# x of the first half stored as its two parts: the low part formed at the eviction in attention, four loads more, one exponential buffer fewer

## The chip, the cores and the metric

One core of one Trainium2 chip runs the whole kernel in one launch. The metric is the device time in microseconds (us) of an execution, the median of three runs unless said otherwise. The engines are TensorE (PE; PEld is its weight load), VectorE (DVE), ScalarE (ACT), GpSimd (POOL) and SyncE (SP). SP does nothing here but issue DMAs, in the order in which they are written; ACT issues a few as well.

## The reference, cut to what matters

```
scores = scale * q @ k.T                        # 4 batches, 12 heads, 448 x 448, head width 64
scores = einsum('bhij,hg->bgij', scores, w_pre)
attn = softmax(scores, axis=-1)
attn = einsum('bhij,hg->bgij', attn, w_post)
x = (attn @ v) as 1792 tokens x 768
h = ((x @ w1) * (x @ w2)) @ w3 @ w_out          # width 1024
out = relu(h @ w_in) ** 2 @ w_out2              # width 2048
```

All of it is float32. The kernel keeps that precision on TensorE by splitting an operand into a rounded high part and a low part (the operand less its high part) and adding three products, high with high, high with low and low with high.

## The kernel before, in words

**Attention.** The rows of the 4 batches are cut into 16 chunks n of 110, 110, 110 and 118 rows, and these into 180 blocks g of up to 10 rows with all 12 heads (120 partitions). A step d of the program handles two blocks, 2d and 2d+1. For them `regroup` loads r (the scores of a block, by a DMA that SP issues two steps ahead), `premix` multiplies r by the mixing weights into PSUM (sp, two buffers, so a step's premix waits until the exponentials of the step before have read theirs), `rowmax` on DVE finds the negated maximum nm, `expo` on ACT takes the exponential p with its sum sm, POOL and DVE turn the sum into a factor (`norm_add`, `norm_recip`), `p_hi` on ACT and `p_lo` on DVE (one step later) make the two halves ph and pl, `tmix` on PE mixes heads (two steps later), and its result is evicted into p2 by ACT (`p2_act`, every fourth block) or DVE (`p2_dve`). When all blocks of chunk n are there, `pv` multiplies by v: two results per chunk, y = 0 and 1, two or three steps apart, in one PSUM buffer. In the step after, `pv_out` on ACT copies the result into a tile xs (three buffers) and SP stores it into xd, a scratch tensor in DRAM that holds x.

The order is written out by hand: `ORDER` lists what each engine does in a step, one line per engine.

```
    ORDER = (
        ("premix", "scores", "tmix", "pv"),
        ("expo", "evac", "p_hi", "p2_act", "pv_out", "high_q"),
        ("rowmax", "p_lo", "norm_recip", "p2_dve", "high_k"),
        ("norm_add", "low_q", "low_k"),
    )
```

**The tail and the layers behind it.** The layers use x in halves of two batches; the first half is chunks n = 0 to 7, with a tile pair (x0h, x0l) for each of its two batches t. The last steps of attention (the tail, numbered by half steps from step 82, `TAIL`) fetch and split the first weights and also x of the first half: `load_x` loads xd into x0l, two chunks in each DMA, and `split_x` makes x0h on ACT (L695) and subtracts it on POOL (L697), in place. For batch t = 1 both come in the last steps. `early` runs the first layer's products of batch 0 on PE between the last steps (e). The second half is loaded and split much later, and the change leaves that as it is.

Of the kernel before, what the change touches and what calls it, by code (L numbers as in the profile page):

```python
# [20 lines left out]
IC = 118  # L21
# [15 lines left out]
def fused_kernel(ctx, tc, q, k, v, w_pre, w_post, w1, w2, w3t, wo, win, wo2, eye, out):  # L37
# [7 lines left out]
    dram = ctx.enter_context(tc.tile_pool(name="dram", bufs=1, space=bass.MemoryType.DRAM))  # L45
    xd = dram.tile([B, 128, 6, S], F, name="xd")
    w34d = dram.tile([6, 128, 8, 128], F, name="w34d")
    w12d = dram.tile([2, 8, 128, DM], F, name="w12d")
# [113 lines left out]
    class Attention:  # L162
        def __init__(self, const, ka, kb, kc, ps):
# [4 lines left out]
            self.nm, self.sm, self.tp, self.p2 = {}, {}, {}, {}  # L168
            self.v, self.pvt = {}, {}
            c = const  # L170
# [31 lines left out]
        def setup_post(self):  # L202
            kw, kab, ones = (self.kc.tile([120, S], F, tag="p", name=x, bufs=5) for x in ("kw", "kab", "ones"))
            kw, kab = (x[:, :120].rearrange("p (g i) -> p g i", i=10) for x in (kw, kab))
# [119 lines left out]
        def expo(self, g):  # L324
            kk = 12 * blocks[g][4]
            if g % 2 == 0:
                self.sm[g // 2] = self.kc.tile([120, 2], F, tag="sm", name=f"sm{g}", bufs=3)
            p = self.kc.tile([120, S], F, tag="p", name=f"p{g}", bufs=5)
            nc.scalar.activation(  # L329
                p[:kk], self.sp.pop(g)[:kk], AF.Exp, bias=self.nm.pop(g)[:kk],  # L330
                accum_out=self.sm[g // 2][:kk, g % 2 : g % 2 + 1],
            )
            self.pt[g] = p
# [103 lines left out]
        def pv_out(self, n, y):  # L437
            o, ic, _ = CHUNKS[n % 4]
            t = self.pvt.pop((n, y))
            u = self.kb.tile([128, 3, IC], F, tag="xs", name=f"xs{n}_{y}", bufs=3)  # L440
            for z, w in ((0, ic),) if ic % 10 == 0 else ((0, 109), (109, 9)):
                nc.scalar.activation(u[:, :, z : z + w], t[:, :, z + z % 10 // 9 : z + z % 10 // 9 + w], AF.Copy)
            eng = nc.sync if n < 15 else nc.scalar
            eng.dma_start(xd[n // 4, :, 3 * y : 3 * y + 3, o : o + ic], u[:, :, :ic])


    TAIL = {
        "w": (-6, -5, -4, -3, 3, 5, 7, 9, 11, 13, 15), "n": (-1, 1, 3, 5, 7, 9, 11, 13, 17),
        "x": (-12, 4), "xn": (0, 11), "h": 8, "hn": 2,
    }  # L450

    def attention_plan():
# [32 lines left out]
        ("expo", "evac", "p_hi", "p2_act", "pv_out", "high_q"),  # L485
        ("rowmax", "p_lo", "norm_recip", "p2_dve", "high_k"),
        ("norm_add", "low_q", "low_k"),
    )
    NEEDS = {
        "rowmax": "premix", "expo": "rowmax", "evac": "scores", "norm_add": "expo", "norm_recip": "norm_add",  # L490
        "p_hi": "norm_recip", "p2_act": "tmix", "p2_dve": "tmix",
    }
# [4 lines left out]
    }  # L497
    AFTER = {"pv_out": "pv", "low_q": "high_q", "low_k": "high_k"}

# [27 lines left out]
    class Moe:  # L527
# [76 lines left out]
        def tail_plan(self):  # L604
# [3 lines left out]
            def at(t, f):  # L608
                ev.setdefault(t, []).append(f)

            for i in range(11):
# [3 lines left out]
                if i < 8:  # L615
                    for part in range(2):
                        at(TAIL["n"][i] + 2, lambda i=i, part=part: w.join(i, part))
                    at(TAIL["n"][i] + 4, lambda i=i: (w.place(i), w.high(i), w.save(i, self.keep[i]), w.rest(i)))
            for u in range(8):
                at(TAIL["x"][u // 4] + 2 * (u % 4), lambda u=u: self.load_x(0, u))  # L620
                at(TAIL["xn"][u // 4] + 2 * (u % 4), lambda u=u: self.split_x(0, u))
            return ev

        def early(self, i, psum):

            ws = [self.w.out[2 * i + j] for j in range(2)]
            xh, xl = self.xy["x", 0, 0]
            assert all((0, u) in self.ready for u in range(4))
            acc = psum(i)
            terms = [(self.chunk(ws, c), (xh[:, c], xl[:, c])) for c in range(6)]  # L630
            for c in range(6):
                yield mm3(acc, terms[c : c + 1], c == 0, c == 5)
            self.acc[i] = acc

        def begin(self, ap_):
            self.ap = ap_

            for c in range(8):
# [30 lines left out]
        def new_xy(self, name, t, parts="hl"):  # L669
            out = []  # L670

            for e, lead, size in (("h", 16, 32), ("l", 48, 96)) if t else (("h", 56, 104), ("l", 24, 32)):
                if e not in parts:
# [6 lines left out]
        def load_x(self, hf, u):  # L680
            t, u4 = divmod(u, 4)
            if u4 == 0:
                part = hf == 0 and t == 0
                self.xy["x", hf, t] = (None, *self.new_xy("x0", t, "l")) if part else self.new_xy(f"x{hf}", t)
            if u4 % 2 == 0:
                w = slice(CHUNKS[u4][0], sum(CHUNKS[u4 + 1][:2]))
                nc.sync.dma_start(f32(self.xy["x", hf, t][1][:, :, w]), xd[2 * hf + t, :, :, w])

        def split_x(self, hf, u):
            t, u4 = divmod(u, 4)  # L690
            o, ic, _ = CHUNKS[u4]
            if self.xy["x", hf, t][0] is None:
                self.xy["x", hf, t] = (*self.new_xy(f"x{hf}", t, "h"), self.xy["x", hf, t][1])
            xh, xl = (x[:, :, o : o + ic] for x in self.xy["x", hf, t])
            nc.scalar.activation(xh, f32(xl), AF.Copy)  # L695
            eng = nc.gpsimd if u % 2 or not hf else nc.vector
            eng.tensor_tensor(xl, f32(xl), f32(xh), ALU.subtract)  # L697
            self.ready.add((hf, u))

# [345 lines left out]
```

## Time and profile before

| what | before |
|---|---|
| median of 3 runs, us | 1312.99 (1311.14 to 1314.83) |
| time of the profiled execution, us | 1316.63 |
| its span, first to last instruction, us | 1314.7 |
| PE busy | 1284.7 us, 98% of the span |
| DVE, ACT, POOL busy | 64%, 55%, 36% |
| granted TensorE clock, mean | 0.996 |

The profiled execution lies 3.6 us above the median, within some 2 us of the slowest of the runs. Its span leaves 1.9 us outside the first and the last instruction. Attention takes the first 460 us of it, the layers the rest. Times in the profile's rows count from the start of the span.

### The profile page before, as it was taken

Reading aid. Unit: us, or ns where it says so; the run is one execution under the profiler, and the core shown is the slowest. Engines: PE = TensorE matmul, PEld = TensorE weight load, DVE = VectorE, ACT = ScalarE, POOL = GpSimd, SP = SyncE. Lnnn points to the kernel's source line nnn. Section 1 sums busy time; section 2 is a strip of 40 time slices with the busy share of each in tenths; the row PEclk is TensorE's granted clock in tenths of the full one; section 3 lists DMA queues with packets and bytes.
Section 4 is the critical chain, followed back from the end, with each engine's and each line's share of the span. In section 5 each row is a group of like instructions: output and inputs, shape, how many; then the busy total and the mean of one; then the engine's idle time right before and its main releaser. Section 6 shows DMA issues by size and latency. Waiting matters only on the chain.

```text
span 1314.7 us, 23355 instructions
## 1 busy us (share of the span) xinstructions
PE 1284.7 (98%) x8542; PEld 1112.2 (85%) x8542; DVE 845.5 (64%) x1535; ACT 716.8 (55%) x1587; POOL 472.8 (36%) x528
## 2 busy tenths in 40 slices
PE   7999999999998999999999999999999999999998
PEld 3677777776766798999999999999999999999998
DVE  4889888889788676643127734769665337735742
ACT  5988889888886565443224533534344225534530
POOL 4354264255324512002222322236776322322331
PEclk9999999999998999999999999999999999999999
DMA  6566576566566567655123432472221223433441
GB/s 213 166 182 191 135 204 205 138 189 204 141 176 185 166 210 219 226 160 153 56 81 108 144 109 75 125 230 91 82 73 48 72 85 111 158 93 86 127 146 52
DMA packets 99399, 184.51 MB, mean 140 GB/s; under 512 B 20949, under 2 KB 68053, under 8 KB 98773
## 3 DMA queue, kind: packets, MB, share of 16 engines
q1 hardware_dynamic: 86928, 172.98, 44.4%
q10 hardware_dynamic: 12357, 10.04, 2.3%
q8 instruction: 67, 1.10, 0.3%
q14 instruction: 47, 0.39, 0.1%
HBM read 124.01 MB, written 20.45 MB: 110 GB/s over the span
## 4 chain that ended last, share of the span: by engine, by line
PE 83%; issue 4%; DVE 4%; DMA 3%; ACT 3%; POOL 2%; SPq 0%; ACTq 0%; POOLq 0%; DVEq 0%
PE l L57 39%; PE y L57 9%; PE sp L315 8%; PE tp L380 5%; PE p L57 5%; PE pv L432 5%; PE sc L289 4%; DMA r<-s 1%; DVE pl L371 1%; DMA kraw<-k 1%; POOL wl L142 1%; ACT ph L355 1%; DVE p L394 1%; DVE nm L321 1%; ACT p L329 1%
## 5 line engine op out<-in xcount | busy, mean ns | idle before, releaser
L142 POOL TENSOR_TENSOR wl<-f,wh 128x384 fp32r<-128x384 f32 (+1 forms) x144 | 166.3, 1155 | 467.2 <-ACT wh L114 446.9
L98 DVE TENSOR_SCALAR f<-y 128x384 int32<-128x384 int32 (+1 forms) x176 | 135.1, 767 | 87.7 <-ACT y L86 86.0
L315 PE MATMUL sp<-r,kpre 120*120 120x448 f32 x360 | 159.8, 565 | 11.4 <-ACT p L329 7.0
L329 ACT ACTIVATE p<-sp,nm 120x448 f32<-120x448 f32 x180 | 113.6, 642 | 49.7 <-DVE nm L321 49.5
L57 PE MATMUL l<-bhh,wh 128*128 128x448 f32 x384 | 139.3, 363 | 0.0
L57 PE MATMUL l<-blh,wh 128*128 128x448 f32 x384 | 138.8, 362 | 0.0
L57 PE MATMUL l<-bhh,wl 128*128 128x448 f32 x384 | 138.7, 361 | 0.0
L371 DVE SCALAR_TENSOR_TENSOR pl<-p,sm,ph 120x448 f16<-120x448 f32 (+3 forms) x270 | 137.6, 563 | 0.3 <-POOL ph L357 0.3
L321 DVE TENSOR_REDUCE nm<-sp 120x1 f32<-120x448 f32 x180 | 107.5, 617 | 42.3 <-PE sp L315 37.7
L114 ACT ACTIVATE wh<-f 128x384 fp32r<-128x384 f32 (+1 forms) x160 | 89.9, 562 | 75.6 <-DVE f L100 68.7
L100 DVE SCALAR_TENSOR_TENSOR f<-raw,f 128x384 int32<-128x384 int32 (+1 forms) x176 | 124.5, 707 | 6.0
L380 PEld LDWEIGHTS <-ph 120*128 120x128 f16 x1260 | 93.7, 99 | 31.9 <-issue 23.9
L355 ACT ACTIVATE ph<-p,sm 120x448 f16<-120x448 f32 (+1 forms) x180 | 107.8, 664 | 17.5 <-DVE sm L349 16.0
L380 PE MATMUL tp<-kwh,ph 120*128 120x120 f16 x630 | 107.0, 218 | 4.5 <-DVE p L396 2.3
L380 PE MATMUL tp<-kwh,pl 120*128 120x120 f16 x630 | 106.1, 217 | 0.0
L380 PE MATMUL tp<-kwl,ph 120*128 120x120 f16 x630 | 106.1, 217 | 0.0
L315 PEld LDWEIGHTS sp<-r,kpre 120*120 120x120 f32 x360 | 59.3, 185 | 54.9 <-issue 19.9
L86 ACT ACTIVATE y<-raw 128x384 f32<-128x384 f32 (+1 forms) x176 | 102.9, 585 | 0.7 <-DMA raw<-w 0.6
L289 PE MATMUL sc<-kt,qh 128*110 128x448 f32 (+1 forms) x192 | 98.4, 512 | 2.2 <-DVE kt L253 1.4
L344 POOL TENSOR_SCALAR sm<-sm 120x2 f32<-120x2 f32 (+3 forms) x94 | 24.7, 263 | 204.9 <-ACT p L329 200.4
L895 ACT ACTIVATE r<-l 128x448 f32<-128x448 f32 x64 | 34.9, 545 | 110.2 <-PE l L57 110.2
L300 ACT ACTIVATE s<-sc 110x448 f32<-110x448 f32 (+1 forms) x186 | 90.5, 559 | 6.2 <-PE sc L289 6.0
(622 smaller groups left out, 3280.9 us busy)
## 6 DMA issues: line engine op xcount, KB each, us to landing
r<-s SPq DMA_DIRECT2D x172, 210.0 KB
raw<-win SPq DMA_DIRECT2D x64, 384.0 KB
raw<-wo SPq DMA_DIRECT2D x48, 512.0 KB
raw<-w SPq DMA_DIRECT2D x32, 384.0 KB
kraw<-k SPq DMA_DIRECT2D x24, 448.0 KB
raw<-w3t SPq DMA_DIRECT2D x16, 512.0 KB
qraw<-q SPq DMA_DIRECT2D x35, 220.0 KB
v<-v SPq DMA_DIRECT2D x4, 1536.0 KB
```

What stands on the lines that cost most here:

```text
L57: nc.tensor.matmul(acc, w, x, start=(first and i == 0 and j == 0), stop=(last and i == n - 1 and j == 2), skip_group_check=again,)
L86: nc.scalar.activation(y, self.raw[i][:, :, 1].bitcast(F), AF.Prelu, scale=2.0**-112, alpha=-(2.0**32))
L98: nc.vector.tensor_scalar(fi, yi, 3, None, ALU.logical_shift_left)
L100: nc.vector.scalar_tensor_tensor(fi, raw[:, :, 0], 29, fi, ALU.logical_shift_right, ALU.bitwise_or)
L142: eng.tensor_tensor(self.out[i][1], self.ft.pop(i), f32(self.out[i][0]), ALU.subtract)
L289: nc.tensor.matmul(sc[:ic], t[:, hh * ic : hh * ic + ic], self.kt[b, h // 2][:, h % 2], start=(i == 0), stop=(i == 1))
L315: nc.tensor.matmul(t[:kk], self.kpre[:kk, :kk], self.rt.pop(g)[:kk], start=True, stop=True)
L321: nc.vector.tensor_reduce(nm[:kk], self.sp[g][:kk], AX.X, ALU.max, negate=True)
L329: nc.scalar.activation(p[:kk], self.sp.pop(g)[:kk], AF.Exp, bias=self.nm.pop(g)[:kk], accum_out=self.sm[g // 2][:kk, g % 2 : g % 2 + 1],)
L355: nc.scalar.activation(h[:, to], p[:, fr], AF.Copy, scale=sm)
L371: nc.vector.scalar_tensor_tensor(l[:, to], p[:, fr], sm, h[:, to], ALU.mult, ALU.subtract)
L380: nc.tensor.matmul(t[:, j], p[:, at : at + 128], w, start=(i == 0), stop=(i == 2))
```

## The change: what it does

For n below 8 `pv_out` writes the rounded high part into xs and a new `pv_lo` on DVE subtracts it from the PSUM result and so makes the low part; SP stores the high part into xd and the low part into a new scratch tensor xld. `pv_lo` is last in DVE's line of the step, and in chunks of 118 rows it takes two instructions, as `pv_out` does. An xs tile now holds both parts (two buffers instead of three). `split_x` is gone for the first half; `load_part` loads x0l from xld and x0h from xd, eight DMAs instead of four, at new places in the tail. The exponentials p have four buffers instead of five. (L numbers in the rows of after are some 1 to 20 higher for the same code.)

```diff
@@ -44,6 +44,7 @@
 
     dram = ctx.enter_context(tc.tile_pool(name="dram", bufs=1, space=bass.MemoryType.DRAM))
     xd = dram.tile([B, 128, 6, S], F, name="xd")
+    xld = dram.tile([B // 2, 128, 6, S], F, name="xld")
     w34d = dram.tile([6, 128, 8, 128], F, name="w34d")
     w12d = dram.tile([2, 8, 128, DM], F, name="w12d")
 
@@ -166,7 +167,7 @@
             self.kt, self.kraw, self.qraw, self.qh, self.ql = {}, {}, {}, {}, {}
             self.st, self.rt, self.sp, self.pt = {}, {}, {}, {}
             self.nm, self.sm, self.tp, self.p2 = {}, {}, {}, {}
-            self.v, self.pvt = {}, {}
+            self.v, self.pvt, self.xs = {}, {}, {}
             c = const
             self.eye = c.tile([120, 10], F, name="eye")
             self.w2a = c.tile([120, 12], F, name="w2a")
@@ -200,7 +201,7 @@
 
 
         def setup_post(self):
-            kw, kab, ones = (self.kc.tile([120, S], F, tag="p", name=x, bufs=5) for x in ("kw", "kab", "ones"))
+            kw, kab, ones = (self.kc.tile([120, S], F, tag="p", name=x, bufs=4) for x in ("kw", "kab", "ones"))
             kw, kab = (x[:, :120].rearrange("p (g i) -> p g i", i=10) for x in (kw, kab))
             ones = ones[:, :128]
             nc.vector.memset(ones, 1.0)
@@ -325,7 +326,7 @@
             kk = 12 * blocks[g][4]
             if g % 2 == 0:
                 self.sm[g // 2] = self.kc.tile([120, 2], F, tag="sm", name=f"sm{g}", bufs=3)
-            p = self.kc.tile([120, S], F, tag="p", name=f"p{g}", bufs=5)
+            p = self.kc.tile([120, S], F, tag="p", name=f"p{g}", bufs=4)
             nc.scalar.activation(
                 p[:kk], self.sp.pop(g)[:kk], AF.Exp, bias=self.nm.pop(g)[:kk],
                 accum_out=self.sm[g // 2][:kk, g % 2 : g % 2 + 1],
@@ -436,17 +437,30 @@
 
         def pv_out(self, n, y):
             o, ic, _ = CHUNKS[n % 4]
-            t = self.pvt.pop((n, y))
-            u = self.kb.tile([128, 3, IC], F, tag="xs", name=f"xs{n}_{y}", bufs=3)
-            for z, w in ((0, ic),) if ic % 10 == 0 else ((0, 109), (109, 9)):
-                nc.scalar.activation(u[:, :, z : z + w], t[:, :, z + z % 10 // 9 : z + z % 10 // 9 + w], AF.Copy)
+            t = self.pvt[n, y]
+            u = self.xs[n, y] = self.kb.tile([128, 2, 3, IC], R, tag="xs", name=f"xs{n}_{y}", bufs=2)
+            for to, fr in self.held(n):
+                nc.scalar.activation((u if n < 8 else f32(u))[:, 0, :, to], t[:, :, fr], AF.Copy)
             eng = nc.sync if n < 15 else nc.scalar
-            eng.dma_start(xd[n // 4, :, 3 * y : 3 * y + 3, o : o + ic], u[:, :, :ic])
+            eng.dma_start(xd[n // 4, :, 3 * y : 3 * y + 3, o : o + ic], f32(u[:, 0, :, :ic]))
+
+        def held(self, n):
+            if n % 4 < 3:
+                return [(slice(0, 110), slice(0, 110))]
+            return [(slice(0, 109), slice(0, 109)), (slice(109, 118), slice(110, 119))]
+
+        def pv_lo(self, n, y):
+            o, ic, _ = CHUNKS[n % 4]
+            t, u = self.pvt.pop((n, y)), self.xs.pop((n, y))
+            if n < 8:
+                for to, fr in self.held(n):
+                    nc.vector.tensor_tensor(u[:, 1, :, to], t[:, :, fr], f32(u[:, 0, :, to]), ALU.subtract)
+                nc.sync.dma_start(xld[n // 4, :, 3 * y : 3 * y + 3, o : o + ic], f32(u[:, 1, :, :ic]))
 
 
     TAIL = {
         "w": (-6, -5, -4, -3, 3, 5, 7, 9, 11, 13, 15), "n": (-1, 1, 3, 5, 7, 9, 11, 13, 17),
-        "x": (-12, 4), "xn": (0, 11), "h": 8, "hn": 2,
+        "x": (-12, 0, 6, 10), "h": 8, "hn": 2,
     }
 
     def attention_plan():
@@ -483,19 +497,19 @@
     ORDER = (
         ("premix", "scores", "tmix", "pv"),
         ("expo", "evac", "p_hi", "p2_act", "pv_out", "high_q"),
-        ("rowmax", "p_lo", "norm_recip", "p2_dve", "high_k"),
+        ("rowmax", "p_lo", "norm_recip", "p2_dve", "high_k", "pv_lo"),
         ("norm_add", "low_q", "low_k"),
     )
     NEEDS = {
         "rowmax": "premix", "expo": "rowmax", "evac": "scores", "norm_add": "expo", "norm_recip": "norm_add",
-        "p_hi": "norm_recip", "p2_act": "tmix", "p2_dve": "tmix",
+        "p_hi": "norm_recip", "p2_act": "tmix", "p2_dve": "tmix", "pv_lo": "pv_out",
     }
 
     LAG = {
         "premix": 0, "tmix": 2, "p2_act": 2, "p2_dve": 2, "rowmax": 0, "expo": 0,
         "norm_add": 0, "norm_recip": 0, "p_hi": 0, "p_lo": 1,
     }
-    AFTER = {"pv_out": "pv", "low_q": "high_q", "low_k": "high_k"}
+    AFTER = {"pv_out": "pv", "pv_lo": "pv", "low_q": "high_q", "low_k": "high_k"}
 
     def attention_step(A, d, ev):
         now, before = ev.get(d, {}), ev.get(d - 1, {})
@@ -616,16 +630,17 @@
                     for part in range(2):
                         at(TAIL["n"][i] + 2, lambda i=i, part=part: w.join(i, part))
                     at(TAIL["n"][i] + 4, lambda i=i: (w.place(i), w.high(i), w.save(i, self.keep[i]), w.rest(i)))
-            for u in range(8):
-                at(TAIL["x"][u // 4] + 2 * (u % 4), lambda u=u: self.load_x(0, u))
-                at(TAIL["xn"][u // 4] + 2 * (u % 4), lambda u=u: self.split_x(0, u))
+            for t in range(2):
+                for k, e in enumerate("lh"):
+                    for u in range(2):
+                        at(TAIL["x"][2 * t + k] + 2 * u, lambda t=t, u=u, e=e: self.load_part(t, u, e))
             return ev
 
         def early(self, i, psum):
 
             ws = [self.w.out[2 * i + j] for j in range(2)]
-            xh, xl = self.xy["x", 0, 0]
-            assert all((0, u) in self.ready for u in range(4))
+            xl, xh = self.xy["x", 0, 0]
+            assert all((0, u, e) in self.ready for u in range(2) for e in "hl")
             acc = psum(i)
             terms = [(self.chunk(ws, c), (xh[:, c], xl[:, c])) for c in range(6)]
             for c in range(6):
@@ -634,6 +649,8 @@
 
         def begin(self, ap_):
             self.ap = ap_
+            for t in range(2):
+                self.xy["x", 0, t] = self.xy["x", 0, t][::-1]
 
             for c in range(8):
                 for e in range(2):
@@ -669,7 +686,7 @@
         def new_xy(self, name, t, parts="hl"):
             out = []
 
-            for e, lead, size in (("h", 16, 32), ("l", 48, 96)) if t else (("h", 56, 104), ("l", 24, 32)):
+            for e, lead, size in (("h", 48, 96), ("l", 16, 32)) if t else (("h", 56, 104), ("l", 24, 32)):
                 if e not in parts:
                     continue
                 p = self.pre if t == 0 and e == "l" else self.wp
@@ -680,22 +697,18 @@
         def load_x(self, hf, u):
             t, u4 = divmod(u, 4)
             if u4 == 0:
-                part = hf == 0 and t == 0
-                self.xy["x", hf, t] = (None, *self.new_xy("x0", t, "l")) if part else self.new_xy(f"x{hf}", t)
+                self.xy["x", hf, t] = self.new_xy(f"x{hf}", t)
             if u4 % 2 == 0:
                 w = slice(CHUNKS[u4][0], sum(CHUNKS[u4 + 1][:2]))
                 nc.sync.dma_start(f32(self.xy["x", hf, t][1][:, :, w]), xd[2 * hf + t, :, :, w])
 
-        def split_x(self, hf, u):
-            t, u4 = divmod(u, 4)
-            o, ic, _ = CHUNKS[u4]
-            if self.xy["x", hf, t][0] is None:
-                self.xy["x", hf, t] = (*self.new_xy(f"x{hf}", t, "h"), self.xy["x", hf, t][1])
-            xh, xl = (x[:, :, o : o + ic] for x in self.xy["x", hf, t])
-            nc.scalar.activation(xh, f32(xl), AF.Copy)
-            eng = nc.gpsimd if u % 2 or not hf else nc.vector
-            eng.tensor_tensor(xl, f32(xl), f32(xh), ALU.subtract)
-            self.ready.add((hf, u))
+        def load_part(self, t, u2, e):
+            if u2 == 0:
+                self.xy["x", 0, t] = (*self.xy.get(("x", 0, t), ()), *self.new_xy("x0", t, e))
+            w = slice(CHUNKS[2 * u2][0], sum(CHUNKS[2 * u2 + 1][:2]))
+            to, src = self.xy["x", 0, t][-1], {"h": xd, "l": xld}[e]
+            nc.sync.dma_start(f32(to[:, :, w]), src[t, :, :, w])
+            self.ready.add((t, u2, e))
 
         def big(self, name):
             return tuple(
```

**On DVE**, around the first eviction of chunk 7 (`xs7_0`; sm is a step's factor, p28 the tile of chunk 7 that `p2_dve` fills, nm98 and nm99 the maxima of the next step's two blocks). Before:

```order
L349 RECIPROCAL sm96_3817<-sm96_3817 120x2
L394 TENSOR_SCALAR p28_3768<-tp93_3797,iv_90 128x36x10
L396 TENSOR_TENSOR p28_3768<-tp93_3797,ivm_91 128x12x20
L321 TENSOR_REDUCE nm98_3877<-sp98_3840 120x1
L321 TENSOR_REDUCE nm99_3879<-sp99_3842 120x1
```

After:

```order
L350 RECIPROCAL sm96_3848<-sm96_3848 120x2
L395 TENSOR_SCALAR p28_3799<-tp93_3828,iv_91 128x36x10
L397 TENSOR_TENSOR p28_3799<-tp93_3828,ivm_92 128x12x20
L457 TENSOR_TENSOR xs7_0_3863<-pv7_0_3756,xs7_0_3863 128x3x109
L457 TENSOR_TENSOR xs7_0_3863<-pv7_0_3756,xs7_0_3863 128x3x9
L322 TENSOR_REDUCE nm98_3911<-sp98_3874 120x1
```

The subtraction reads the xs tile that ACT writes in the same step, and stands in front of the next step's maxima.

**On ACT**, the same place after (p97 the step's last exponential, p98 the next step's first):

```order
L356 ACTIVATE ph0_87<-p96_3849,sm96_3848 120x448
L356 ACTIVATE ph0_87<-p97_3851,sm96_3848 120x384
L393 ACTIVATE p28_3799<-tp92_3818,iv_91 128x36x10
L443 ACTIVATE xs7_0_3863<-pv7_0_3756 128x3x109
L443 ACTIVATE xs7_0_3863<-pv7_0_3756 128x3x9
L330 ACTIVATE p98_3919,sm98_3918<-sp98_3874,nm98_3911 120x448
```

Nothing moved here: the eviction stands where it stood, behind both ph and the eviction of tmix.

**On SP**, the steps 82 to 84 of the tail (r168 to r173 are the scores of blocks 168 to 173; blocks 170 and 171 are premixed in step 85, 172 and 173 in step 86). Before:

```order
L307 DMA r169_6308<-s15_5942 120x1x448
L444 DMA xd_57<-xs13_0_6357 128x3x110
L307 DMA r170_6369<-s15_5942 120x1x448
L307 DMA r171_6371<-s15_5942 120x1x448
L307 DMA r172_6452<-s15_5942 120x1x448
L307 DMA r173_6454<-s15_5942 120x1x448
L444 DMA xd_57<-xs13_1_6503 128x3x110
```

After:

```order
L308 DMA r169_6345<-s15_5979 120x1x448
L445 DMA xd_57<-xs13_0_6394 128x3x110
L710 DMA x0h0_6403<-xd_57 128x6x220
L308 DMA r170_6405<-s15_5979 120x1x448
L308 DMA r171_6407<-s15_5979 120x1x448
L710 DMA x0h0_6403<-xd_57 128x6x228
L308 DMA r172_6487<-s15_5979 120x1x448
L308 DMA r173_6489<-s15_5979 120x1x448
```

Two loads of x0h (660 and 684 KB) now stand ahead of the two pairs of r.

## Rows read from the trace of the kernel before

**Rows 1.** Busy time by stretch: PE, PEld, DVE, ACT, POOL; clock, DMA share, GB/s

```profile
160.00:264.00 104.00, 102.75 (x1057) 75.74 (x1057) 89.86 (x204) 89.89 (x222) 45.25 (x71) 1.00 0.62 181
400.00:417.50 17.50, 14.25 (x150) 9.49 (x148) 14.32 (x32) 12.29 (x29) 5.92 (x9) 1.00 0.37 125
417.50:424.50 7.00, 5.87 (x31) 3.82 (x33) 6.96 (x12) 5.52 (x13) 5.30 (x6) 0.51 0.90 226
440.00:462.00 22.00, 20.38 (x246) 18.11 (x244) 11.79 (x21) 9.07 (x22) 12.56 (x9) 1.00 0.33 96
```

**Rows 2.** Chain of waits, 160 to 260 us: shares by line, and one piece

```profile
by line: PE sp L315 27.5%; PE tp L380 19.3%; PE pv L432 17.3%; PE sc L289 14.2%; DMA kraw<-k 6.0%; DVE pl L371 3.5%; ACT ph L355 2.2%; DVE nm L321 2.2%; issue 1.5%; SPq L307 1.2%; ACT s L300 1.1%; DVE p L394 1.0%; ACT p L392 0.9%; ACT p L32
...
200.49 2.41 PE pv L432 x48
```

**Rows 3.** Timeline at chunk 7, y = 0: start, duration, engine, line (DVE, ACT, PE)

```profile
247.78 1.14 DVE L321 TENSOR_REDUCE nm<-sp 120x1 f32<-120x448 f32 x2
...
247.15 1.18 ACT L355 ACTIVATE ph<-p,sm 120x448 f16<-120x448 f32 x2 [0.73 <-DVE sm L349]
248.24 0.55 ACT L392 ACTIVATE p<-tp,iv 128x360 f32<-128x360 f32 x1
248.68 0.51 ACT L442 ACTIVATE xs<-pv 128x327 f32<-128x327 f32 x2
...
249.86 0.64 PE L315 MATMUL sp<-r,kpre 120*120 120x448 f32 x1
```

**Rows 4.** Timeline at chunk 1, y = 1 (ACT, DVE, PE)

```profile
108.10 0.42 ACT L442 ACTIVATE xs<-pv 128x330 f32<-128x330 f32 x1
...
108.15 1.14 DVE L321 TENSOR_REDUCE nm<-sp 120x1 f32<-120x448 f32 x2
...
109.64 0.63 PE L315 MATMUL sp<-r,kpre 120*120 120x448 f32 x1
```

**Rows 5.** Groups of instructions: busy us, mean ns of one, idle before, releaser

```profile
L697 POOL TENSOR_TENSOR x0l<-x0l,x0h 128x660 fp32r<-128x660 f32 x6 | 11.8, 1964 | 4.6 <-ACT x0h L695 4.5
...
L881 DVE TENSOR_TENSOR y0l<-y,y0h 128x448 fp32r<-128x448 f32 x12 | 7.5, 625 | 44.3 <-ACT y0h L880 44.3
...
L695 ACT ACTIVATE x0h<-x0l 128x660 fp32r<-128x660 f32 x6 | 4.5, 748 | 0.0
```

**Rows 6.** Timeline of DVE and POOL in the tail

```profile
402.32 1.40 DVE L371 SCALAR_TENSOR_TENSOR pl<-p,sm,ph 120x448 f16<-120x448 f32 x3
...
417.08 3.43 DVE L371 SCALAR_TENSOR_TENSOR pl<-p,sm,ph 120x448 f16<-120x448 f32 x3
...
418.05 1.85 POOL L697 TENSOR_TENSOR x0l<-x0l,x0h 128x660 fp32r<-128x660 f32 x1
```

**Rows 7.** Who waited for whom, whole span: us in total, times, longest

```profile
PE sp L315 <- DMA r<-s: 4.2, 5, 1.6
```

**Rows 8.** Chain of waits, 376 to 395 us: from a DMA's issue to its landing

```profile
378.29 6.28 DMA r<-s
...
386.17 8.42 DMA r<-s
```

**Rows 9.** Timeline of SP and PE, steps 76 to 86 of the tail

```profile
377.58 0.62 SPq L687 DMA_DIRECT2D x0l<-xd  x1
378.29 4.02 SPq L307 DMA_DIRECT2D r<-s  x4
...
406.36 3.41 SPq L307 DMA_DIRECT2D r<-s  x4
...
412.67 0.64 PE L315 MATMUL sp<-r,kpre 120*120 120x448 f32 x1 [1.10 <-ACT p L329]
...
418.63 3.34 PE L315 MATMUL sp<-r,kpre 120*120 120x448 f32 x4 [1.64 <-ACT p L329]
```

**Rows 10.** DMA view, 406.4 to 411.5 us: busy tenths in 40 slices of 0.13 us

```profile
DMA  0006988840066656666676666666666567666610
```

**Rows 11.** DMA view, 864 to 879 us, where x of the second half is loaded

```profile
DMA packets 3788, 4.58 MB, mean 305 GB/s; under 512 B 127, under 2 KB 3454, under 8 KB 3788
```

## The prediction

> **What bounds the kernel now.** I read the busy time by stretch first, then the chain of waits, then the timelines at the places that the change touches. In the attention of the first half PE is busy nearly all the time: 102.75 of 104 us between 160 and 264 us, while DVE stands at 89.86 and ACT at 89.89 [rows 1]. The chain of waits says the same: three quarters of it is PE's matmuls (27.5 + 19.3 + 17.3 + 14.2%) [rows 2]. So DVE has about a seventh of its time free, but it isn't far behind PE: what holds up a row maximum holds up the exponential, and the next step's premix waits for that one's PSUM buffer. The tail is looser. From 400 to 417.5 us PE lacks 3.25 us (17.5 less 14.25); from 417.5 to 424.5 it works at a clock of 0.51, the lower level of 1.2 GHz, after the waits before it; from 440 to 462 it lacks 1.62 [rows 1]. There ACT and POOL split x, and the change works there. Behind 462 us nothing in the layers is altered.
>
> **What goes.** Eight copies on ACT of 0.75 us and eight subtracts on POOL of 1.96 us (the two for the wider chunks are alike) [rows 5]. They cost more than their own time: a step's three `p_lo` take 1.40 us where POOL is quiet and 3.43 us where the 1.85 us subtract runs beside them [rows 6]. The most that all this can give back is what PE lost in the three stretches of the tail: 3.25 us, 1.62 us, and in the slow stretch 1.13 us idle (7.00 less 5.87) and about half of the 5.87 us at half clock, 2.9 us. That is 8.9 us.
>
> Beside the row on `p_lo` stands a rule: the Trainium skill, "SBUF — State Buffer", section "Who interferes with whom", says that a DVE instruction with two SBUF inputs and a GpSimd instruction that reads SBUF exclude each other, and that the later one waits for the whole of the other. The rows agree in kind: 3.43 less 1.40 is 2.03, beside a subtract of 1.85. By it alone all eight subtracts could come off DVE's path, and the gain would tend to the 8.9 us.
>
> **What comes, on DVE.** Sixteen times, once for each of the two results of chunks 0 to 7, `pv_lo` stands at the end of a step's DVE work, and it reads the xs tile that ACT writes in that step. Its price is bounded by the nearest row, 625 ns for 448 columns with one input from PSUM [rows 5]; for 330 columns in proportion 0.46 us. I take 0.42 us until the next instruction can start, since the rows of DVE overlap their neighbours by some 0.05 to 0.1 us, and 0.57 us with the second piece in chunks 3 and 7.
>
> The wait is dearer than the work. At chunk 7, y = 0, DVE is ready for the next row maxima at 247.78. ACT, though, first makes ph (1.18 us from 247.15), then evicts tmix (0.55), then xs, which ends at 248.68 + 0.51 = 249.19 [rows 3]. DVE now waits 1.41 us for it, takes 0.1 us to hear of it, subtracts for 0.57, and the maximum starts at 249.86. From a maximum's start to the premix that its exponential releases I take 1.45 us: at chunk 1 it is 108.15 to 109.64, 1.49 us, in a place where ACT waited for the maximum [rows 4]. So the premix of 249.86 [rows 3] comes at 251.31, 1.45 us late. At chunk 1, y = 1, ACT has no eviction of tmix in front: xs ends at 108.52, 0.37 us after DVE is free; the maximum comes at 109.04 and the premix at 110.5 in place of 109.64 [rows 4], 0.9 us late. Where a pv of 2.41 us [rows 2] stands on PE in front of that premix, it hides the delay; this is so at the first result of chunks 0, 2, 3 and 5. Read in this way, the sixteen places give, chunk by chunk (y = 0 / y = 1): 0 / 0.4, 1.1 / 0.9, 0 / 1.2, 0 / 1.0, 0.4 / 0.8, 0 / 0.4, 0.4 / 0.4, 1.45 / 0.7. That is 9.2 us in sum. PE stands in the middle of its own chain at these places, so I count them as lost. I take off 1.2 us, since in some of these steps DVE waits 0.2 to 0.5 us for the factor in any case and makes up as much: **8.0 us**, between 3 (half of the places absorbed by the 14% that DVE has free) and 11 (DVE stays behind from one place to the next).
>
> **What comes, on SP.** Sixteen stores into xld stand right behind those into xd, and SP waits for `pv_lo` there, about 0.7 us longer than for xs, and needs some 0.4 us to issue. Queued behind it are the loads of r two steps ahead, of q and of k. PE waited for r only five times, 4.2 us in all [rows 7], so most of this is covered by the lead of r; without that cover it would be up to 1 us at each place. I take 0.5 us, from 0 to 2.
>
> **Four exponential buffers: nothing.** The exponential of a step now needs the buffer of two steps before. Its last reader, `p_lo`, stands on DVE ahead of the row maximum for which that exponential waits anyway.
>
> **What comes, in the tail.** Two loads of x0h stand ahead of the r of steps 85 and 86. Now, the four DMAs of r issued from 406.36 on [rows 9] run on the DMA engines from slice 12 to slice 38, 407.8 to 411.3 us [rows 10]; the first pair is thus in at about 409.5, 3.2 us after its issue. Behind an x load it took 6.28 and 8.42 us [rows 8, 9], so such a load costs the r behind it 3.1 to 5.2 us. A lower bound comes from the second half's loads: 305 GB/s with other traffic [rows 11] makes 660 KB 2.2 us. By the Trainium skill, "DMA: Bandwidth & Descriptors", section "Specifications", which gives 358 GB/s per core from HBM, it would be an estimated 1.9 us, and r nearly as early as now. I take 3.1 us, the nearest row: it is the same load ahead of the same r. Then the r of step 85 is in at 412.6, where premix 85 now starts at 412.67, and that of step 86 at 411.3 + 6.2 = 417.5, premix 86 now at 418.63 [rows 9]. What ACT and POOL give back before 418 us is so taken up by r, the idle time in front of the slow stretch stays about as it is, and with it, I think, the lower clock. There remains the end, 440 to 462 us, where the loads of x0h for t = 1 have nothing but weights behind them: of the 1.62 us I count 1.5 back. The tail gives **-1.5 us**, between -7 (a load costs 2.2 us, premix 86 comes 2.6 us earlier, the 2.9 us at the lower clock fall away) and +3 (5.2 us each: r of step 86 at 421.7).
>
> **The sum.** 8.0 + 0.5 - 1.5 = +7.0 us on the profiled execution's 1316.63, 1323.6. It lies 3.6 us above the median of 1312.99, so the median should go to **1320.0**.
>
> **The rivals.** A change of 0.3% is 3.9 us, about what a measurement of this kernel tells from none.
>
> *A, `pv_lo` is hidden.* DVE's free seventh takes it: 16 times about 1.5 us of wait and work are 24 us over 200 us in which DVE has some 27 us free. For it: the sum fits. Against it: the wait falls in front of the maxima, not where DVE idles. First half +2, tail -1.5: 1313.5.
>
> *B, faster: the tail is freed.* Place: the steps from 400 to 424 us. Without x0l on POOL the three `p_lo` fall from 3.43 to 1.40 us [rows 6], premixes 85 and 86 come early, PE doesn't idle, and the clock stays at its higher level (2.4 GHz). Its price is -8.9 us at most, -8 with the loads in time; it decides if an x load costs r less than about 2.2 us and the first half less than 4: 1312.99 + 3.5 - 8 = 1308.5. Against it: the two rows of 6.28 and 8.42 us. The rule of the Trainium skill on the shared port, given above, speaks for it.
>
> *C, slower still.* The loads collide as in the dearer row (+3), DVE stays behind (+10), and SP's longer queue delays k at the batch changes (+1): 1327.
>
> **How the numbers follow.** The forecast gets 0.52, A 0.20, B 0.18, C 0.10. Slower by over 0.3% (above 1316.9) are the forecast and C, 0.62; A is within, 0.20; B faster, 0.18. The forecast's own range, with 3 to 11, 0 to 2 and -7 to +3, each not at its end at once, is 1315 to 1325. For 8 in 10 I go down to 1309, which leaves out about half of B, and up to 1326, which leaves out about half of C.
>
> **What would show it.** Right: in the first half DVE's `pv_lo` waits for ACT's xs, by 0.3 to 1.4 us each time, and premix waits for the exponential right behind it; the last premix of chunk 7 comes some 8 us later than now. In the tail premix 85 and 86 wait for r instead of for ACT, and a stretch at the lower clock remains. Wrong: `pv_lo` without idle time ahead of it, PE as busy as now up to 264 us, or a tail that is shorter by 5 us or more. The forecast falls if PE had slack that its busy time hides, or if the queue lets r pass an x load.

## The result, and the profile after

The changed kernel takes 1320.55 us (median of 6 runs, 1319.07 to 1324.37), the kernel before 1314.05 in the same series (6 runs, 1311.14 to 1315.14): ratio 1.0055, 95% interval 1.0042 to 1.0067. The change makes it slower by 6.5 us. The forecast was 1320.0, in a range of 1309 to 1326. The profiled execution after took 1322.03 us (span 1320.2).

The busy time by stretch, kernel after, columns as in [rows 1]:

```profile
160.00:264.00 104.00, 99.64 (x1025) 72.98 (x1024) 88.59 (x206) 86.50 (x212) 45.62 (x68) 1.00 0.65 188
400.00:417.50 17.50, 15.49 (x173) 11.74 (x171) 13.54 (x34) 12.39 (x29) 2.76 (x8) 0.90 0.79 215
417.50:424.50 7.00, 6.54 (x64) 3.95 (x60) 5.22 (x12) 3.97 (x10) 0.79 (x3) 1.00 0.86 252
445.50:467.50 22.00, 21.27 (x254) 18.88 (x254) 10.99 (x21) 7.52 (x20) 4.96 (x6) 1.00 0.54 169
```

In the first half PE now lacks 4.36 us of 104, before 1.25 [rows 1]. In the last 22 us ahead of the layers, which here begin 5.5 us later, it lacks 0.73 in place of 1.62. Who waited, kernel after, 60 to 270 us (first two rows) and 384 to 450 us (last):

```profile
DVE xs L457 <- ACT xs L443: 14.0, 14, 1.5
...
PE sp L316 <- ACT p L330: 7.5, 13, 1.3
...
PE sp L316 <- DMA r<-s: 5.0, 5, 1.9
```

The place of [rows 3] (chunk 7, y = 0), kernel after:

```profile
252.94 0.55 ACT L393 ACTIVATE p<-tp,iv 128x360 f32<-128x360 f32 x1
253.39 0.51 ACT L443 ACTIVATE xs<-pv 128x327 fp32r<-128x327 f32 x2
253.93 0.59 DVE L457 TENSOR_TENSOR xs<-pv,xs 128x327 fp32r<-128x327 f32 x2 [1.36 <-ACT xs L443]
254.44 1.15 DVE L322 TENSOR_REDUCE nm<-sp 120x1 f32<-120x448 f32 x2
255.09 0.63 ACT L330 ACTIVATE p<-sp,nm 120x448 f32<-120x448 f32 x1 [1.19 <-DVE nm L322]
...
255.86 1.76 PE L316 MATMUL sp<-r,kpre 120*120 120x448 f32 x4 [1.16 <-ACT p L330]
```

The chain reads down the rows: ACT's copy ends at 253.90, DVE has stood for 1.36 us and now subtracts, the row maximum starts at 254.44, the exponential at 255.09, and PE, idle for 1.16 us, gets its buffer at 255.86.

To place the loss I take three marks in each trace: the first premix of step 12 (78.29 us before, 77.19 after), that of step 54 (269.50 and 276.24), and the first matmul of the layers that isn't an early one, `l<-x0h` (461.62 and 467.15). The first half, mark 1 to 2, went from 191.21 to 199.05, **+7.84**; the stretch from mark 2 to 3, called the tail from here on though it begins at step 54, from 192.12 to 190.91, **-1.21**. Up to mark 1 the kernel after is 1.10 us ahead, and the layers behind mark 3 differ by less than 0.1. Two cautions. The profiled execution before took 1316.63, 2.6 us over its median, with PE at half clock for 6.8 us of the tail, so the tails of other runs look up to some 2.6 us better against it than the medians say. And a mark is read from a single execution: two kernels below whose edits lie in the tail alone, e4 and e8, have a first half that is 1.6 and 3.7 us longer than that of the kernel they were made from.

One run of e3 (1827.28 us) and one of e12 (4548.72 us), both below, were far slower than all others and are left out of the medians.

### The profile page after: what moved, and what is told of

It reads as the page before. It is cut to its first block, busy times and chain, and to the rows that moved or that the text cites. A ratio compares the mean times of both kernels' runs of the same rounds, so it can differ in the third digit from the quotient of the medians.

```text
span 1320.2 us, 23406 instructions
## 1 busy us (share of the span) xinstructions
PE 1286.2 (97%) x8542; PEld 1111.4 (84%) x8542; DVE 842.1 (64%) x1555; ACT 714.0 (54%) x1579; POOL 460.5 (35%) x520
## 4 chain that ended last, share of the span: by engine, by line
PE 80%; ACT 6%; DVE 4%; DMA 4%; issue 4%; POOL 1%; SPq 0%; ACTq 0%; POOLq 0%; DVEq 0%
PE l L58 39%; PE y L58 9%; PE sp L316 7%; PE p L58 5%; PE pv L433 5%; PE tp L381 4%; PE sc L290 3%; DMA r<-s 3%; ACT p L330 2%; ACT ph L356 2%; DVE nm L322 2%; DMA kraw<-k 1%; ACT s L301 1%; DVE pl L372 1%; POOL wl L143 1%
## 5 line engine op out<-in xcount | busy, mean ns | idle before, releaser
L372 DVE SCALAR_TENSOR_TENSOR pl<-p,sm,ph 120x448 f16<-120x448 f32 (+3 forms) x270 | 129.5, 534 | 0.0
```

Source lines behind the costliest of these rows:

```text
L372: nc.vector.scalar_tensor_tensor(l[:, to], p[:, fr], sm, h[:, to], ALU.mult, ALU.subtract)
```

## The experiments

Each run stands against the kernel before on the same chip, in three series (e1 to e4, e5 to e8, e9 to e12); the median of before was 1314.2 to 1314.4 (17 to 23 runs). "First half" and "tail" are the marks above, in the profiled execution.

| run | median us | ratio to before, 95% interval | first half | tail |
|---|---|---|---|---|
| before | 1314.05 | | 191.21 | 192.12 |
| after | 1320.55 | 1.0055 (1.0042 to 1.0067) | 199.05 | 190.91 |
| e1 low part later | 1318.67 | 1.0030 (1.0018 to 1.0042) | 195.50 | 187.35 |
| e2 copied, not subtracted | 1320.26 | 1.0046 (1.0032 to 1.0059) | 199.03 | 189.87 |
| e3 tail alone | 1312.53 | 0.9982 (0.9973 to 0.9992) | 190.86 | 188.31 |
| e4 x from ACT's queue | 1317.33 | 1.0023 (1.0012 to 1.0033) | 200.62 | 184.03 |
| e5 work, no wait | 1314.87 | 1.0005 (0.9996 to 1.0015) | 193.52 | 188.57 |
| e6 wait, no work | 1314.90 | 1.0001 (0.9991 to 1.0010) | 194.71 | 188.85 |
| e7 low part on POOL | 1325.91 | 1.0084 (1.0069 to 1.0098) | 202.22 | 188.12 |
| e8 e7 and e4 | 1324.55 | 1.0078 (1.0063 to 1.0092) | 205.91 | 184.81 |
| e9 ACT's copy first | 1305.81 | 0.9931 (0.9919 to 0.9944) | 191.04 | 181.27 |
| e10 e9 and e4 | 1304.79 | 0.9930 (0.9916 to 0.9945) | 191.06 | 181.31 |
| e11 before, x from ACT's queue | 1313.04 | 0.9988 (0.9979 to 0.9997) | 190.34 | 187.84 |
| e12 no low store | 1320.07 | 1.0042 (1.0030 to 1.0055) | 197.76 | 187.77 |

**e1, the low part one step later.**

```diff
-        ("rowmax", "p_lo", "norm_recip", "p2_dve", "high_k", "pv_lo"),
+        ("rowmax", "pv_lo", "p_lo", "norm_recip", "p2_dve", "high_k"),
...
+                    elif kind == "pv_lo":
+                        args = ev.get(d - 2, {}).get("pv", [])
```

> Whole change, but DVE forms the low part one step later, behind that step's two row maxima instead of in front of them; the buffer of the PV sum comes free one step later, still before the next PV product is issued. Theory 1 (the 7.8 us that the first half lost are DVE waiting for ACT's copy ahead of the row maxima): 6 to 7 us come back, 1313 to 1315 us, and the low part's wait for ACT falls from 14.0 us under 2 us. Rival (the added DVE work, 16 instructions of about 0.5 us, or the 16 added stores, cost by being there): under 2 us come back, 1319 us or more.

Neither. The wait fell as foreseen, to 1.5 us, but only 1.9 us came back in the medians and 3.6 in the first half. Behind the row maxima the work stands ahead of the factor that ACT's ph needs, and that wait grew. Kernel e1, 60 to 270 us (after: 2.6 us, 4 times):

```profile
ACT ph L356 <- DVE sm L350: 5.3, 11, 1.1
```

The kernel before had 4.1 us of it, though, 7 times, so this can be only part of the 4.3 us that the first half still loses; the rest stays open.

**e2, the same place, copied instead of subtracted.**

```diff
-                    nc.vector.tensor_tensor(u[:, 1, :, to], t[:, :, fr], f32(u[:, 0, :, to]), ALU.subtract)
+                    nc.vector.tensor_copy(u[:, 1, :, to], t[:, :, fr])
```

> The low part of x is not formed: at the same place and with the same stores, DVE copies the PV sum from PSUM instead of subtracting ACT's copy from it, so the instruction stays and its wait for ACT goes. Theory 1 (the wait): 5 to 7 us come back, 1313.5 to 1316 us, since the copy can begin when the PV product ends and 0.4 to 0.57 us of it lie beside the next premix. Rival (the DVE work itself in front of the row maxima, 16 x 0.5 = 8 us): at most 1.5 us come back, 1319 us or more.

The time says "rival", but the experiment didn't do what it says. Who waited, kernel e2, 60 to 270 us:

```profile
DVE xs L457 <- ACT xs L443: 14.0, 14, 1.5
```

The copy still waited for ACT, to the tenth as long as the subtract, so this run tells the theories apart in no way. It shows that copy and subtract cost the same at this place, 199.03 and 199.05 us. e5 and e6 take its place.

**e3, the tail alone.** `pv_lo` and its stores are gone, and the low part's loads read `xd`:

```diff
-            to, src = self.xy["x", 0, t][-1], {"h": xd, "l": xld}[e]
+            to, src = self.xy["x", 0, t][-1], xd
```

> The low part is not formed and not stored; the loads of the low part read the stored high part instead, so the low part of x in the second half is wrong. Left of the change: the loads in the tail, no splits there, four exponential buffers. If the first half's loss is pv_lo's and its stores' and the tail gives 1.2 us: 0.5 to 2 us under the kernel before, 1312 to 1313.5 us. Rival (the four buffers or the new loads cost the first half something): the first half stays longer than before by 1 us or more, 1314.5 us or more.

As expected: 1312.53, and the first half is back at 190.86. So the whole loss there belongs to `pv_lo` and its stores, and the four exponential buffers, which this kernel keeps, cost nothing that the mark shows. The tail by itself is worth 1 to 3.5 us (0.08 to 0.27% by the interval).

**e4, the loads of x from ACT's queue.**

```diff
-            nc.sync.dma_start(f32(to[:, :, w]), src[t, :, :, w])
+            nc.scalar.dma_start(f32(to[:, :, w]), src[t, :, :, w])
```

> Whole change, but the eight loads of x in the tail are issued from ACT's queue instead of SP's, at the same steps. Theory 2 (in the tail the regroup transfers r wait in SP's queue behind the loads of x, which eats what ACT and POOL gave back): the waits of the premixes for r in 384 to 450 us fall from 5.0 us to under 3 us, and 2 to 4 us come back, 1316.5 to 1318.5 us. Rival (the transfers share the DMA engines whichever queue issues them): r lands as late as now, 1320 to 1321.5 us.

As the theory says: 3.2 us back, and PE's waits for r from 384 to 450 us fall from 5.0 to 2.2:

```profile
PE sp L316 <- DMA r<-s: 2.2, 3, 1.5
```

The Trainium skill, "DMA: Bandwidth & Descriptors", section "Issuing engines are not separate DMA queues", says that transfers share the same DMA engines whichever engine issues them, and that a second issuer saves only its sequencer's time. By that rule alone no more than that time would come back, 0.55 to 0.90 us on SP for each of the eight loads in the trace after. The edit changes only the queue that the loads stand in, so the 3.2 us are its doing; how much of them is that time, and how much the place of r behind the loads' data, this run doesn't tell. For the place it speaks that the r of step 85, where PE waited for it, landed 6.53 us after its issue here and 7.1 to 7.9 us after it in e1 to e3 and e5 to e7, which load x from SP's queue.

**e5, the work without the wait.** DVE copies 330 columns of the tmix result that it read last, into a tile of its own:

```diff
-                    nc.vector.tensor_tensor(u[:, 1, :, to], t[:, :, fr], f32(u[:, 0, :, to]), ALU.subtract)
+                    nc.vector.tensor_copy(self.lo[:, :, to], self.last[:, :, ...])
```

> The low part of x is not formed: at the same place, and with the same store, DVE copies as many columns of a tmix result that it has just read, into a tile of its own, so that the instruction has its work but no wait for ACT (the copy of the PV sum in the run before still waited 14.0 us for it). Theory 1 (wait and work in series ahead of the row maxima): the copy is over before the premix result is there, the first half loses under 2 us against before in place of 7.8, 1313.5 to 1316 us. Rival (DVE's work alone): 6 us or more of the loss stay, 1318.5 us or more.

The group of these instructions, kernel after and then kernel e5, 60 to 270 us (busy us, mean ns of one, idle ahead and what ended it):

```profile
L457 DVE TENSOR_TENSOR xs<-pv,xs 128x330 fp32r<-128x330 f32 (+2 forms) x20 | 8.3, 434 | 14.0 <-ACT xs L443 14.0
```

```profile
L459 DVE CAST xl<-tp 128x330 fp32r<-128x330 f32 (+2 forms) x20 | 8.2, 426 | 0.0
```

The same work, no wait: 2.31 us lost in the first half in place of 7.84, a little over the 2 foreseen. The rival falls.

**e6, the wait without the work.** The subtract is made for one column, and not stored:

```diff
...
+                z, f = (slice(x.stop - 1, x.stop) for x in (to, fr))
+                nc.vector.tensor_tensor(u[:, 1, 2:, z], t[:, 2:, f], f32(u[:, 0, 2:, z]), ALU.subtract)
...
```

> The low part of x is formed for one column of each chunk and half only and not stored, the loads of the low part read the high part: the wait for ACT stays in front of the row maxima, with 0.1 us of work in place of 0.42 to 0.57. Theory 1: each delay of the table falls by the work that is gone, 0.4 to 0.5 us, to 0 at the least, so that 2 to 4 us of the 7.8 stay in the first half, 1315 to 1317 us. Rival (the work alone costs): under 1 us stays, 1314 us or less.

3.50 us lost in the first half; the total, 1314.9, lies just under the foreseen range, and its interval reaches into the rival's. Wait and work each alone cost 3.5 and 2.3 us, together 7.84, more than their sum: they stand in series ahead of the maximum, and each alone is partly covered by DVE's free time there. The medians agree: against e3, which has the same tail, e5 and e6 take 2.3 and 2.4 us more.

**e7, the low part on POOL.** ACT copies the sum to SBUF unsplit, and POOL makes both parts and has both stored:

```diff
...
+                nc.gpsimd.tensor_copy(uh, f32(ul))
+                nc.gpsimd.tensor_tensor(ul, f32(ul), f32(uh), ALU.subtract)
...
```

> ACT evacuates the PV sum unsplit to SBUF, and POOL forms both parts there, behind its own work of the step; both are stored as in the change, and the tail is that of the change. Theory: DVE is free of the split, so the first half loses under 2 us against before, 1313 to 1315.5 us. Rival (POOL's work stretches DVE's p_lo, as beside its subtracts in the tail, or keeps norm_add waiting): 4 us or more are lost, 1317 us or more.

The rival's number, 1325.9, but not its mechanism alone. SP's waits, kernel e7, 60 to 384 us, and then DVE's waits for POOL's sum and for k, 60 to 270 us (for k after: 1.9 us, once; before: 3.5 us, 4 times):

```profile
SPq L461 <- POOL xs L458: 56.8, 15, 6.6
SPq L446 <- ACT xs L443: 30.4, 8, 7.5
...
DVE sm L350 <- POOL sm L345: 7.7, 15, 1.5
DVE kt L245 <- DMA kraw<-k: 7.7, 6, 3.1
```

SP stands at the store until POOL is done, 15 times and up to 6.6 us, and what is behind it in the queue comes late: k, and r too, which in steps 12 to 53 is issued on average 6.5 us ahead of its premix (before: 7.9). From 60 to 270 us SP stands for 64 us at its stores in e7 and for 58 in the kernel before, so there is little more of it. What part each has, and what part POOL's own lateness (the third row; after: 2.7 us, 6 times; before: 6.0, 17 times), isn't shown.

**e8, e7 with the loads of x from ACT's queue.**

> The run before this one together with the loads of x from ACT's queue. If the two gains add: 2 to 4 us under that run, 1310 to 1312.5 us, and under the kernel before by 0.15 to 0.35%. Rival (the 3 us of the loads were of the first half's delay, not of the tail): no more than 1 us under that run.

1.4 us under e7, between the two, with overlapping intervals. In the profiles the tail is 3.3 us shorter than e7's, as theory has it, and the first half, which this edit doesn't touch, 3.7 us longer. So the run doesn't decide.

**e9, ACT's copy first.** One line of the whole change:

```diff
-        ("expo", "evac", "p_hi", "p2_act", "pv_out", "high_q"),
+        ("pv_out", "expo", "evac", "p_hi", "p2_act", "high_q"),
```

> Whole change, but ACT copies the PV sum first in the next step, ahead of that step's exponentials, where it waits for the row maxima anyway, instead of behind them: DVE's low part stands where it stood, and finds the copy made. Theory 1 (the wait for ACT's late copy, and only a rest of 2.3 us for the work, as in the run with work and no wait): 4 to 6 us of the 7.8 come back in the first half, 1314.5 to 1317 us. Rival (ACT's 0.54 us ahead of the exponentials delay them as much as they spare DVE): no more than 2 us, 1318.5 us or more.

Better than expected: 1305.81 us, 14.7 under the change and 8.6 (0.69%, interval 0.56 to 0.81) under the kernel before. At chunk 7, y = 0, kernel e9:

```profile
243.78 0.51 ACT L443 ACTIVATE xs<-pv 128x327 fp32r<-128x327 f32 x2
244.29 1.38 DVE L322 TENSOR_REDUCE nm<-sp 120x1 f32<-120x448 f32 x2 [1.38 <-PE sp L316]
244.95 0.63 ACT L330 ACTIVATE p<-sp,nm 120x448 f32<-120x448 f32 x1 [0.65 <-DVE nm L322]
...
247.78 0.58 DVE L457 TENSOR_TENSOR xs<-pv,xs 128x327 fp32r<-128x327 f32 x2
248.28 1.15 DVE L322 TENSOR_REDUCE nm<-sp 120x1 f32<-120x448 f32 x2
```

The copy lies where ACT waits for the row maximum anyway (0.65 us of wait are still left behind it), and DVE's subtract follows its own work with no idle time ahead. The first half is 191.04, no longer than before: all of the loss came back, also the 2.3 us that theory 1 had left for the work, so e5's 2.31 us aren't simply the price of that work. The tail, moreover, is 9.6 us shorter than after's, which theory 1 doesn't give: 1.7 us of it from step 54 to 75, where chunks have no low part but ACT's copy is first too, 2.1 from step 76 to 81, 5.4 from step 82 to 88, and 0.4 behind. SP's waits for these stores, 60 to 384 us, kernel before, kernel after and then kernel e9:

```profile
SPq L444 <- ACT xs L442: 90.1, 24, 6.9
```

```profile
SPq L445 <- ACT xs L443: 91.2, 25, 7.7
```

```profile
SPq L458 <- DVE xs L457: 39.8, 16, 4.0
...
SPq L445 <- ACT xs L443: 16.2, 11, 3.9
...
SPq L445 <- ACT p L330: 3.6, 4, 1.3
SPq L445 <- ACT s L301: 2.8, 3, 1.5
```

In the kernel before SP stood for 90.1 us at its stores, and after for 91.2; now it is 62. What is queued behind is issued earlier: r, counted from its issue on SP to its premix, has on average 8.1 us after and 10.7 in e9 in steps 54 to 75, and 8.3 and 11.0 in steps 76 to 89; in the first half it changes little, 8.0 and 8.2. In the tail no premix waits for r any more; all waits of PE from 384 to 450 us, kernel e9:

```profile
PE tp L381 <- DVE p L397: 0.7, 3, 0.3
PE sp L316 <- ACT p L330: 0.7, 1, 0.7
PE pv L433 <- ACT xs L443: 0.6, 1, 0.6
PE tp L381 <- ACT p L393: 0.5, 2, 0.3
```

**e10, e9 with the loads of x from ACT's queue.**

> The run before this one together with the loads of x from ACT's queue, which alone gave 3.2 us. If both causes are told rightly and lie in different stages, the gains add: 1311.5 to 1314 us, at or under the kernel before. Rival (they draw on the same slack, as on POOL, where the queue gave 1.4 us): 1 us or less under the run before.

The rival: 1304.79, 1.0 us under e9, with intervals that overlap almost wholly, and the same marks. Where r is in time, its place behind x costs nothing.

**e11, the kernel before with its loads of x from ACT's queue.**

> The kernel before with one edit: its four loads of x in the tail come from ACT's queue. Theory 2 (r waits behind the loads of x in SP's queue, in the kernel before too): 1 to 3 us under the kernel before, 1311 to 1313.5 us. Rival (only the change's four further loads hold r up): within 1 us of before.

1313.04, 1.4 us under before, its interval just clear of 1: the figure lies with theory 2, for less than in e4, but the interval, 0.4 to 2.8 us, doesn't shut out the rival.

**e12, no low store.**

> Whole change without the 16 stores of the low part (the loads of the low part read the stored high part, so the second half's low part is wrong): what SP and the DMA engines pay. Prediction: 0.5 us less than the whole change, 1319.5 to 1320.5 us. Rival (the stores hold r and k up behind them on SP): 2 us or more less.

0.5 us under the whole change, as predicted, but no difference that the intervals show.

## Why the prediction was right, point by point

**`pv_lo` in the first half: +8.0 foreseen, +7.84 measured.** The table of delays held place by place. Foreseen, and the growth of the lag from one premix to the next in the trace after:

```
chunk       0        1        2        3        4        5        6        7
foreseen  0/0.4  1.1/0.9   0/1.2    0/1.0   0.4/0.8   0/0.4  0.4/0.4  1.45/0.7
measured  0/0.4  1.1/0.4   0/1.2    0/1.0    0/0.8    0/0.4  0.4/0.4   1.3/0.6
```

At chunk 2, y = 1, the 1.2 us come at two premixes running, 0.60 and 0.57. The 1.2 us taken off as a lump are found at chunks 1, 4 and 7. At chunk 7, y = 0, the parts were a little smaller than taken: DVE began 0.03 us after ACT's copy ended (0.1 taken) and worked 0.51 us (0.57 taken). That this is wait and work in series is shown by e5 and e6; that PE stands in the middle of its chain there, by the last row of the timeline above. Rival A, a hidden `pv_lo`, falls with that: DVE's free seventh lies elsewhere. For the first half it would have been right with ACT's copy first (e9).

**SP's stores, +0.5:** e12 gives 0.5, within its interval of nothing. **Four buffers, 0:** e3 confirms it.

**The tail, -1.5 foreseen, -1.21 measured**, nearly the right sum with wrong places in it. The chain of waits, kernel after, has r at

```profile
386.03 7.37 DMA r<-s
...
430.17 9.70 DMA r<-s
```

and these premixes waited for r, kernel after:

```profile
392.16 0.98 PE L316 MATMUL sp<-r,kpre 120*120 120x448 f32 x2 [1.46 <-DMA r<-s]
393.54 0.98 PE L316 MATMUL sp<-r,kpre 120*120 120x448 f32 x2 [0.39 <-DMA r<-s]
410.97 2.23 PE L316 MATMUL sp<-r,kpre 120*120 120x448 f32 x4 [1.91 <-DMA r<-s]
...
438.03 0.98 PE L316 MATMUL sp<-r,kpre 120*120 120x448 f32 x2 [0.26 <-DMA r<-s]
440.00 0.98 PE L316 MATMUL sp<-r,kpre 120*120 120x448 f32 x2 [0.98 <-DMA r<-s]
```

They are those of steps 79, 83 and 88, and not of 85 and 86 as foreseen: 85 found its r there, and 86 waited 1.0 us for an exponential. In e1 to e3 and e5 to e7, which have the change's loads of x on SP, premix 85 did wait, by 2.0 to 3.3 us; kernel e3:

```profile
412.63 3.14 PE L316 MATMUL sp<-r,kpre 120*120 120x448 f32 x4 [3.33 <-DMA r<-s]
```

So the foreseen wait exists, but not in the trace after, and r was also held up where no load of x stood right ahead of it: ahead of the r of step 83 SP had issued two loads of weights. Next to the 3.2 us without a load ahead [rows 9, 10], the two r of the chain took 4.2 and 6.5 us more, behind a load of x and, at 430.17, a load of weights too; the 3.1 us taken were too few. Against that the stretch at half clock, which I left as it was, shrank from 6.8 to 3.4 us. By the premixes the -1.21 us are -0.53 from step 54 to 81, +0.36 from step 82 to 88, where the balance was foreseen, and -1.05 from premix 89 to the layers, where 1.5 was. That the balance came out by other steps than the foreseen ones is luck. That r takes back what ACT and POOL gave is shown in part by e4, where the loads of x leave SP's queue and 3.2 us come back. Rival B's condition, r in time, is met only in e9 and e10: from premix 82 to the layers e9 takes 55.14 us in place of 61.64 before, which is 6.5 of the 8.9 us.

The rule of the Trainium skill on the shared port ("SBUF — State Buffer", section "Who interferes with whom"), by which all eight subtracts could come off, agrees as to DVE: from 400 to 462 us the group of `p_lo` has a mean of 561 ns after and 778 before:

```profile
L372 DVE SCALAR_TENSOR_TENSOR pl<-p,sm,ph 120x384 f16<-120x384 f32 (+5 forms) x32 | 16.3, 561 | 0.0
```

```profile
L371 DVE SCALAR_TENSOR_TENSOR pl<-p,sm,ph 120x448 f16<-120x448 f32 (+5 forms) x27 | 19.6, 778 | 0.0
```

DVE was freed, and PE waited for r instead.

**What stays open.** How much of e9's 8.6 us under before comes from the copy's place alone, in the kernel before, wasn't tried. That SP's shorter waits at the stores let r be issued earlier fits the rows of e9 and e7, but no run moved the stores by themselves. And the tail of e12 is 3.1 us shorter than that of after for a like total, of which a stretch at half clock in the layers gives back 1.5; a single profile tells such differences only roughly.

## What to carry to other kernels

Before an engine is given work that reads another's output, look where that output stands in the other engine's order: behind the late copy the subtract made this change slow, behind an early one it cost the first half nothing, and one moved entry turned 0.55% slower into 0.69% faster. Put an instruction that two others wait for into the gap where its engine waits anyway, here ahead of the exponentials. A store in SP's queue held everything behind it until its source was ready, here for up to 7.7 us: read that queue's own waits.

## What was not expected of the hardware

PE fell to the lower of its two levels (1.2 GHz) after single waits of 1.9 to 2.0 us, but not after each of them. In the trace after, premix 83 waited 1.91 us for r until 410.97, and from 412.74 to 416.15 the granted clock was at half. In e9 the one such stretch in the layers followed a wait of 2.03 us that ended at 527.55; kernel e9, by stretch:

```profile
520.00:527.50 7.50, 5.52 (x27) 4.88 (x27) 6.07 (x13) 3.51 (x7) 0.00 (x0) 1.00 0.55 182
527.50:531.00 3.50, 3.45 (x11) 3.45 (x12) 3.43 (x7) 2.37 (x5) 0.00 (x0) 0.51 0.65 205
```

It cost 1.5 us: at the third mark e9 lay 10.88 us under before, and 9.35 when the products behind the first layers began; e10, without such a stretch there, kept its 10.87. The same product waits in all 14 traces, 1.89 to 2.04 us long, and half clock followed it in six (e4, e6, e7, e8, e9, e12): there mark 3 to the end takes 854.5 to 854.6 us, in the other eight 853.0 to 853.1. So the wait alone doesn't settle it, and what does isn't shown. Which execution has such a stretch, and where, differs, and that is part of the spread of the times.
